# A causal convolution in 64x32 TensorE tiles, set behind the second product tile of a block

## The chip, the cores and the metric

The kernel runs on one core of one Trainium2 chip. The metric is the device time of one execution in microseconds. Three runs of the kernel before gave 463.99, 464.58 and 464.65, median 464.58. The profile is of one further execution.

The engines are named as in the profile: PE is TensorE (PEld its weight loads), DVE is VectorE, ACT is ScalarE, POOL is GpSimd, and SP issues most DMAs.

## The reference, cut to what matters

```python
# x: (8, 4160, 192)   weight: (8 heads, 7 taps)   group = 192 / 8 = 24
w = softmax(weight, axis=-1)
x_pad = concatenate([zeros((B, 6, D)), x], axis=1)
out[b, s, h, g] = sum_k w[h, k] * x_pad[b, s + k, h, g]        # a causal convolution of 7 taps
y = out.reshape(33280, 192)
h = maximum(maximum(y @ w1, y @ w2), y @ w3)                   # each w: (192, 768)
return h @ w_out                                               # w_out: (768, 192)
```

## The kernel before, in words

**Blocks.** The 33280 tokens are dealt into 65 blocks of 512. A block goes through a convolution that gives y, a first stage that gives h, and a second stage that gives the output. All matmuls are in fp16 with fp32 sums.

**First stage (`l1`, lines 499 to 504).** The maximum of three is taken as w3's product plus max(relu(first - third), second - third): `wd` holds w1 - w3 in its lower 64 rows and w2 - w3 in its upper 64. A block has six product tiles j of 128 hidden columns. For each, three matmuls of 512 columns run on the lower half of the array (rows 0 to 63, into a bank of pool `psp`, tile `lp`) and three on the upper half (rows 64 to 127, pool `psq`, tile `lq`), side by side. ScalarE takes the relu of `lp` into `r` (line 503), and VectorE takes the maximum of `r` and `lq` into `h` (line 504). Each pool has two banks.

**Second stage (`st2`, line 551).** The part of w3 that was taken out is added through `m16` = w3 @ w_out, straight from y. In each half 30 matmuls of 192 columns sum into banks of pool `psw` (four banks, tile `po`); at two places of a block ScalarE copies the lower half's sums (line 560) and VectorE adds the upper half's (line 561). The second stage of block t - 1 is dealt between the product tiles of block t, five matmuls of each half after every one, always lower, upper, lower, upper.

**Convolution.** It is made in three ways. Blocks 0 to 3 use dense matmuls (`conv_dense`, line 415, 112x32 tiles) at the start. Twelve blocks (`qpos`: 11, 16, ... 61 and 64) are made on GpSimd: cast, transposed by DMA, and summed tap by tap (`tap_q`, lines 229 to 240). All others use TensorE with a band matrix of the taps (`conv`, line 397): block 4 alone, the rest in pairs. A load (`load_x`, line 144) brings eight pieces of 70 rows (64 tokens and 6 ahead of them), GpSimd casts them (`cast_x`, line 176), and sixteen matmuls of 70 rows, 64 output tokens and 192 columns (8 heads by two column halves) write four banks, taken from `psw`, `psp`, `psw` and `psq`. Two evacuations on ScalarE and two on VectorE (line 443) copy them into `ys`. A DMA transpose for each block (`turn`, line 454) makes y with channels on partitions, and two DMAs a block (`double`, line 462) copy it to the other half of the partitions, since both halves of the array need it.

**Order.** The schedule is written by hand. In the loop over t, SP gets the load of block t + 6, the doubling of block t + 2, and later the turn of block t + 3 and the store of block t - 2. The pair (u, u + 1) is convolved in block u - 3, after that block's first product tile, behind one second-stage matmul of the lower half that is moved ahead. GpSimd gets the cast of block t + 5 and that block's share of the taps.

Of the kernel before, what the change touches and what calls it, by code (L numbers as in the profile page):

```python
# [14 lines left out]
P = 128  # L15
# [12 lines left out]
def kernel(  # L28
# [42 lines left out]
    qpos = [q for q in range(11, NB - 3, EVERY)] + [NB - 1]  # L71
# [23 lines left out]
    NR = NBLK // HALF  # L95

    def rows_of(t):
        rows = [(b, S + o) for (b, S, N, off) in blocks[t] for o in range(0, N, HALF)]
        assert len(rows) == NR
        return rows  # L100
# [4 lines left out]
    xfp = ctx.enter_context(tc.tile_pool(name="xfp", bufs=6))  # L105
# [5 lines left out]
    ydp = ctx.enter_context(tc.tile_pool(name="ydp", bufs=6))  # L111
# [9 lines left out]
    xin = {}  # L121

    def load_x(t, eng=nc.sync):
        if not 0 <= t < NB or t in qset:
            return
        pool, tag = (xfp, "xf") if t > 1 else ((xap, "xa"), (xbp, "xb"))[t]
        xf = pool.tile([P, NR, D], FP32, tag=tag, name=f"xf_{t}")
        if t < NDENSE:
            todo = [(0, c[3], c[1] * SEQ + c[2]) for c in chunks_of[t]]
        else:  # L130
            todo = [(PAD, HALF, b * SEQ) if s == 0 else (0, HALF + PAD, b * SEQ + s - PAD)
                    for b, s in rows_of(t)]
        parts = []
        i, n = 0, len(todo)
        row = [c[2] for c in todo]
        while i < n:
            k = i
            while k + 1 < n and todo[k + 1][:2] == todo[i][:2] and row[k + 1] - row[k] == row[i + 1] - row[i]:
                k += 1
            step = row[i + 1] - row[i] if k > i else 0  # L140
            p0, rlen = todo[i][:2]
            src = bass.AP(tensor=x.tensor, offset=row[i] * D,
                          ap=[[D, rlen], [step * D, k - i + 1], [1, D]])
            eng.dma_start(out=xf[p0:p0 + rlen, i:k + 1, :], in_=src)
            if parts and parts[-1][0] == rlen:
                parts[-1] = (rlen, parts[-1][1], k + 1)
            else:
                parts.append((rlen, i, k + 1))
            i = k + 1
        xin[t] = [xf, todo[0][0], parts]  # L150
# [14 lines left out]
    def cast_x(t):  # L165
# [4 lines left out]
        if u == 0:  # L170
            x16s[t0] = x16p.tile([P, NHEAD, 2, nu, NR // 2, GRP], FP16, tag="x16", name=f"x16_{t0}")
        if p0:
            nc.gpsimd.memset(xf[0:p0, 0, :], 0.0)
        K = HALF + PAD
        for c in range(2):
            nc.gpsimd.tensor_copy(out=x16s[t0][0:K, :, c, u, :, :].rearrange("p h r c -> p r h c"),  # L176
                                  in_=xf[0:K, c:NR:2, :].rearrange("p r (h c) -> p r h c", c=GRP))


# [41 lines left out]
    def tap_q(q, k):  # L221
# [17 lines left out]
        yd = dense[q] = ydp.tile([P, 2, NCH // 2, P], FP16, tag="yd", name=f"yd_{q}")  # L239
# [41 lines left out]
    for t in range(2, 7):  # L281
        load_x(t)

# [3 lines left out]
    nc.gpsimd.tensor_copy(out=ident16[:], in_=ident[:])  # L287
    idle = const.tile([P, NBLK], FP16)
# [25 lines left out]
    for v in range(2):  # L314
        nc.gpsimd.memset(xz[1][v][:], 0.0)
    wcol16 = const.tile([P, 3, KW], FP16)
# [70 lines left out]
    def conv(t, pools):  # L387
# [4 lines left out]
        per = NHEAD // n  # L392
        w = nu * (NR // 2) * GRP
        G = [pool.tile([P, per, w], FP32, tag=tag, name=f"G{i}_{t}") for i, (pool, tag) in enumerate(pools)]
        for h in range(NHEAD):
            for c in range(2):
                nc.tensor.matmul(  # L397
                    G[h // per][HALF * c:HALF * (c + 1), h % per, :],
                    lhsT=band[0:HALF + PAD, h, PAD:HALF + PAD],
                    rhs=x16s[t0][0:HALF + PAD, h, c, :, :, :].rearrange("p u r c -> p (u r c)"),  # L400
                    start=True, stop=True, tile_position=(0, HALF * c))
        slots[t0] = ysp.tile([P, nu, NR // 2, D], FP16, tag="ys", name=f"ys_{t}")
# [35 lines left out]
    def evac(t, i, copy=nc.scalar.copy):  # L438
# [3 lines left out]
        per = NHEAD // len(G)  # L442
        copy(out=slots[t][:, :, :, GRP * per * i:GRP * per * (i + 1)].rearrange(  # L443
# [3 lines left out]
    def turn(t):  # L447


        if t >= NB or t in qset:  # L450
            return
        t0, u, nu = place(t)
        yd = dense[t] = ydp.tile([P, 2, NCH // 2, P], FP16, tag="yd", name=f"yd_{t}")
        nc.sync.dma_start_transpose(out=yd[:, 0, :, :],
                                    in_=slots[t0][:, u, :, :].rearrange("p r d -> p (r d)"))

    def double(t):

        if NDENSE <= t < NB:
            yd = dense[t]  # L460
            for i in range(2):
                nc.sync.dma_start(out=yd[HALF * i:HALF * (i + 1), 1, :, :],
                                  in_=yd[HALF * (1 - i):HALF * (2 - i), 0, :, :])

    def spot(t, i, c, r):
# [3 lines left out]
        else:  # L469
            own, k = (NC * r + c) % 2, (NC * r + c) // 2  # L470
        return k + (0 if own == i else NCH // 2)

    def y_all(t, i, c):
        row = slice(HALF * i, HALF * (i + 1))
        if t < NDENSE:
            return dense[t][row, c, :]
        a = dense[t][row, 0, 0, :]
# [5 lines left out]
    def y_tok(t, i, c, s):  # L483
        row = slice(HALF * i, HALF * (i + 1))
        if t < NDENSE:
            return dense[t][row, c, P * s:P * (s + 1)]
        k = spot(t, i, c, s)
        return dense[t][row, k // 6, k % 6, :]

    def l1(t, j, pools=((psp, "p"), (psq, "q"))):  # L490


        N = blkN[t]
        ps = [pool.tile([P, NBLK], FP32, tag=tag, name=f"l{tag}{i}_{t}_{j}")
              for i, (pool, tag) in enumerate(pools)]
        for c in range(NC):
            for i in range(2):
                row = slice(HALF * i, HALF * (i + 1))
                nc.tensor.matmul(ps[i][:, 0:N], lhsT=wd[row, c, P * j:P * (j + 1)],  # L499
                                 rhs=y_all(t, i, c),  # L500
                                 start=(c == 0), stop=(c == NC - 1))
        r = rp.tile([P, NBLK], FP16, tag="r", name=f"r_{t}_{j}")
        nc.scalar.activation(out=r[:, 0:N], in_=ps[0][:, 0:N], func=AF.Relu)  # L503
        nc.vector.tensor_max(out=hs[t][:, j, 0:N], in0=r[:, 0:N], in1=ps[1][:, 0:N])  # L504

    ahead = set()

    def st2(t, u, NU, first_half_only=False):
# [5 lines left out]
        hT = hs[t]  # L514
        if t not in halves:
            todo = [[], []]
            for s in range(4):
                for i in range(2):
                    row = slice(HALF * i, HALF * (i + 1))
                    mm = [(y_tok(t, i, i, s), m16[row, 0, :])]  # L520
                    if s % 2 == i:
                        mm.append((y_tok(t, i, 2, s), m16[row, 1, :]))
                    hh = [(hT[row, j, P * s:P * (s + 1)], wo[row, j, :]) for j in range(NJ)]
                    mm = hh + mm if t == 0 else mm + hh
                    todo[i] += [(s, n == 0, n == len(mm) - 1, m) for n, m in enumerate(mm)]
# [6 lines left out]
            halves[t] = (todo, {})  # L532
        todo, ps = halves[t]
        n = len(todo[0])
        es = range(n * u // NU, n * (u + 1) // NU)
        for e in es[:1] if first_half_only else es:
            for i in range(2):
                if first_half_only:
                    if i:
                        break  # L540
                    ahead.add((t, e))
                elif i == 0 and (t, e) in ahead:
                    continue
                s, first, last, (a, b) = todo[i][e]
                b0 = s if t == NB - 1 else s - s % 2
                if (b0, i) not in ps:
                    pool, tag = (psw, "w")
                    if t == NB - 1 and s in (1, 2):
                        pool, tag = (psp, "p") if i == 0 else (psq, "q")
                    ps[b0, i] = pool.tile([P, 2, D], FP32, tag=tag, name=f"po{i}_{t}_{s}")  # L550
                nc.tensor.matmul(ps[b0, i][:, s % 2, :], lhsT=a, rhs=b, start=first, stop=last)  # L551
            ends = {todo[i][e][0] for i in range(2) if todo[i][e][2]}
            for s in sorted(ends):
                done[t, s] = done.get((t, s), 0) + sum(todo[i][e][0] == s and todo[i][e][2] for i in range(2))
                if done[t, s] < 2 or (s % 2 == 0 and t < NB - 1):
                    continue
                s0 = s if t == NB - 1 else s - 1
                ss = slice(s0 % 2, s % 2 + 1)
                a = tp.tile([P, 2, D], FP32, tag="a", name=f"a_{t}_{s}")
                nc.scalar.copy(out=a[:, ss, :], in_=ps[s0, 0][:, ss, :])  # L560
                nc.vector.tensor_add(out=outs[t][:, s0:s + 1, :], in0=a[:, ss, :],  # L561
                                     in1=ps[s0, 1][:, ss, :])
                if t == NB - 1 and s == 1:
                    store(t, 0, 2, (nc.sync,))
                elif t == NB - 1 and s == 3:
                    store(t, 2, 3, (nc.scalar,))
                    store(t, 3, 4, (nc.sync,))
# [17 lines left out]
    def begin(t):  # L585
        hs[t] = hp.tile([P, NJ, NBLK], FP16, tag="h", name=f"h_{t}")
# [168 lines left out]
```

## Time and profile before

| | |
|---|---|
| profiled execution | 464.5 us, its span 462.7 us |
| median of three runs | 464.58 us |
| granted TensorE clock | 1.00 |
| a second-stage matmul (line 551), 64x192 | 3120 and 780 of them, 243 ns as recorded |
| a first-stage matmul (line 499), 64x512 | 2316 in `lp` and `lq`, 376 ns as recorded |
| relu (line 503), maximum (line 504) | 597 ns, 686 ns |
| evacuation of the convolution (line 443) | 484 ns on ScalarE, 550 ns on VectorE, 49 each |
| GpSimd: one tap's product (229), sum (237), a cast (176) | 478 ns, 1809 ns, 822 ns |

[...] matmuls that follow each other overlap in the record: how close they start tells their cost, not how long each is. The two halves of the array are independent rows of the same timeline. The share of idle time of an engine says little unless TensorE waits for it.

### The profile page before, as it was taken

Reading aid. Unit: us, or ns where it says so; the run is one execution under the profiler, and the core shown is the slowest. Engines: PE = TensorE matmul, PEld = TensorE weight load, DVE = VectorE, ACT = ScalarE, POOL = GpSimd, SP = SyncE. Lnnn points to the kernel's source line nnn. Section 1 sums busy time; section 2 is a strip of 40 time slices with the busy share of each in tenths; the row PEclk is TensorE's granted clock in tenths of the full one; section 3 lists DMA queues with packets and bytes.
Section 4 is the critical chain, followed back from the end, with each engine's and each line's share of the span. In section 5 each row is a group of like instructions: output and inputs, shape, how many; then the busy total and the mean of one; then the engine's idle time right before and its main releaser. Section 6 shows DMA issues by size and latency. Waiting matters only on the chain.

```text
span 462.7 us, 17259 instructions
## 1 busy us (share of the span) xinstructions
PE 454.4 (98%) x6969; PEld 367.9 (80%) x6969; DVE 354.1 (77%) x595; ACT 314.3 (68%) x597; POOL 352.6 (76%) x501
## 2 busy tenths in 40 slices
PE   8999999999999999999999999999999999999997
PEld 4576788977877887888888888888888888888886
DVE  6777777777778787777878777777777777777775
ACT  5766566667676666767667676676767676676664
POOL 5753289999988978978967978978957969979500
PEclk9999999999999999999999999999999999999999
DMA  8959999999869878787789697698598797884423
GB/s 190 222 127 198 177 209 179 192 209 224 192 130 231 170 155 211 175 181 183 166 175 198 157 211 165 157 213 198 132 210 179 164 224 176 144 191 92 100 70 103
DMA packets 137527, 80.77 MB, mean 175 GB/s; under 512 B 58294, under 2 KB 137368, under 8 KB 137448
## 3 DMA queue, kind: packets, MB, share of 16 engines
q1 hardware_dynamic: 137176, 79.18, 79.1%
q8 instruction: 54, 0.88, 0.9%
q0 software_dynamic: 112, 0.39, 0.3%
q14 instruction: 25, 0.20, 0.2%
q10 hardware_dynamic: 160, 0.10, 0.1%
HBM read 29.85 MB, written 25.56 MB: 120 GB/s over the span
## 4 chain that ended last, share of the span: by engine, by line
PE 89%; POOL 5%; DMA 4%; issue 1%; DVE 0%; ACT 0%; POOLq 0%; DVEq 0%; SPq 0%
PE lq L499 35%; PE po L551 33%; PE lp L499 14%; PE G L397 4%; POOL tap L237 2%; POOL tap L229 2%; DMA yd<-ys 1%; PE idle L294 1%; DMA xt<-xq 1%; DMA yd<-yd 1%; PE D L415 1%; POOL x L176 1%; DMA xt<-xt 1%; PE lw L499 0%; PE band_cols L335 0%
## 5 line engine op out<-in xcount | busy, mean ns | idle before, releaser
L504 DVE TENSOR_TENSOR h<-r,lq 128x512 f16<-128x512 f16 x386 | 264.7, 686 | 99.5 <-ACT r L503 99.4
L503 ACT ACTIVATE r<-lp 128x512 f16<-128x512 f32 x386 | 230.5, 597 | 134.7 <-PE lp L499 123.8
L499 PE MATMUL lp<-yd,wd 64*128 64x512 f16 x1158 | 312.3, 376 | 2.2 <-DMA yd<-yd 1.6
L499 PE MATMUL lq<-yd,wd 64*128 64x512 f16 x1158 | 312.3, 376 | 0.3 <-DVE yd L431 0.3
L551 PE MATMUL po<-wo,h 64*128 64x192 f16 x3120 | 263.8, 243 | 0.7 <-issue 0.7
L551 PEld LDWEIGHTS <-h 64*128 64x128 f16 x3120 | 209.2, 94 | 22.2 <-issue 0.9
L499 PEld LDWEIGHTS <-wd 64*128 64x128 f16 x2340 | 160.9, 94 | 39.4 <-DMA yd<-yd 2.1
L176 POOL CAST x<-xf 70x768 f16<-70x768 f32 x98 | 77.8, 822 | 60.6 <-DMA xf<-in_x_dram 54.0
L229 POOL TENSOR_SCALAR tap<-xt,wcol 128x256 f32<-128x256 f16 x252 | 116.1, 478 | 3.9 <-DMA xt<-xt 3.3
L237 POOL TENSOR_TENSOR tap<-tap,tap 128x768 f32<-128x768 f32 x60 | 108.6, 1809 | 5.0
L551 PE MATMUL po<-m,yd 64*128 64x192 f16 x780 | 109.4, 243 | 0.0
L561 DVE TENSOR_TENSOR o<-a,po 128x384 f32<-128x384 f32 (+1 forms) x132 | 71.4, 541 | 1.2 <-ACT a L560 1.2
L551 PEld LDWEIGHTS <-yd 64*128 64x128 f16 x780 | 61.9, 94 | 11.8
L560 ACT COPY a<-po 128x384 f32<-128x384 f32 (+1 forms) x132 | 62.3, 473 | 3.0 <-PE po L551 3.0
L443 DVE CAST ys<-G 128x384 f16<-128x384 f32 x49 | 24.9, 550 | 0.6 <-PE G L397 0.6
L397 PEld LDWEIGHTS <-band 70*64 70x64 f16 x400 | 15.8, 109 | 9.9 <-PE lp L499 9.0
L240 POOL TENSOR_TENSOR yd<-tap,tap 128x768 f16<-128x768 f32 x12 | 21.8, 1814 | 1.0
L397 PE MATMUL G<-x,band 70*64 70x192 f16 (+1 forms) x400 | 21.2, 248 | 0.7 <-POOL x L176 0.5
L443 ACT CAST ys<-G 128x384 f16<-128x384 f32 x49 | 21.0, 484 | 0.8 <-PE G L397 0.8
L198 POOL CAST xq<-xl 128x384 f16<-128x384 f32 x24 | 11.4, 505 | 0.0
L256 POOL CAST xz<-xf 112x80 f16<-112x80 f32 (+2 forms) x18 | 5.2, 330 | 4.5 <-DMA xf<-in_x_dram 4.5
L294 PE MATMUL idle<-idle 128*128 128x512 f16 x15 | 6.4, 573 | 1.2 <-DVE idle L289 1.2
(52 smaller groups left out, 68.6 us busy)
## 6 DMA issues: line engine op xcount, KB each, us to landing
out_dram<-o SPq DMA_DIRECT2D x61, 384.0 KB
xf<-in_x_dram SPq DMA_DIRECT2D x47, 420.0 KB
yd<-yd SPq DMA_DIRECT2D x122, 96.0 KB
xl<-in_x_dram SPq DMA_DIRECT2D x12, 384.0 KB
xf<-in_x_dram SPq DMA_DIRECT2D x5, 367.5 KB
ws<-in_moe_w_dram SPq DMA_DIRECT2D x6, 192.0 KB
out_dram<-o SPq DMA_DIRECT2D x5, 192.0 KB
yd<-ys SPq DMA_TRANSPOSE x49
```

The lines of the kernel that those rows point to most:

```text
L176: nc.gpsimd.tensor_copy(out=x16s[t0][0:K, :, c, u, :, :].rearrange("p h r c -> p r h c"), in_=xf[0:K, c:NR:2, :].rearrange("p r (h c) -> p ...
L229: nc.gpsimd.tensor_scalar(out=part[:, 2 * c:2 * c + 2, :], in0=xt[:, 2 * c:2 * c + 2, LEAD - PAD + k:LEAD - PAD + k + P], scalar1=wcol[:, ...
L237: nc.gpsimd.tensor_add(out=accs[q][:], in0=accs[q][:], in1=part[:])
L240: nc.gpsimd.tensor_add(out=yd[:, 0, :, :], in0=accs.pop(q)[:], in1=part[:])
L397: nc.tensor.matmul(G[h // per][HALF * c:HALF * (c + 1), h % per, :], lhsT=band[0:HALF + PAD, h, PAD:HALF + PAD], rhs=x16s[t0][0:HALF + PAD ...
L443: copy(out=slots[t][:, :, :, GRP * per * i:GRP * per * (i + 1)].rearrange("p u r (h c) -> p h (u r) c", c=GRP), in_=G[i][:].rearrange("p h ...
L499: nc.tensor.matmul(ps[i][:, 0:N], lhsT=wd[row, c, P * j:P * (j + 1)], rhs=y_all(t, i, c), start=(c == 0), stop=(c == NC - 1))
L503: nc.scalar.activation(out=r[:, 0:N], in_=ps[0][:, 0:N], func=AF.Relu)
L504: nc.vector.tensor_max(out=hs[t][:, j, 0:N], in0=r[:, 0:N], in1=ps[1][:, 0:N])
L551: nc.tensor.matmul(ps[b0, i][:, s % 2, :], lhsT=a, rhs=b, start=first, stop=last)
L560: nc.scalar.copy(out=a[:, ss, :], in_=ps[s0, 0][:, ss, :])
L561: nc.vector.tensor_add(out=outs[t][:, s0:s + 1, :], in0=a[:, ss, :], in1=ps[s0, 1][:, ss, :])
```

## The change

- `conv`: the sixteen matmuls become 64. The array is used as 64x32 tiles: two row halves and four column quarters. A matmul now has 38 rows (32 tokens and 6 ahead of them), 32 output tokens and 96 columns for a pair of blocks. A block is loaded as sixteen pieces of 38 rows, eight on partitions 0 to 37 and eight on 64 to 101, so a load is two DMAs. The cast covers 102 partitions; the rows between are set to zero once, in six buffers that are now fixed ones.
- `turn`: two transposes for a pair, both issued behind the pair's evacuation; `double`: two DMAs for a pair instead of four. In SP's order the doubling now comes before the load.
- The convolution of a pair stands behind the second product tile. In such a block the second stage is dealt 5, 8, 4, 4, 5, 4 (`ROOM`) instead of five each: three (`OWN`) of the eight stand before the convolution in the upper half, and four more (`AHEAD`) in the lower half.
- TensorE's instructions go through two queues in the program, one for each half (`mm`, `emit`), and are written in the order in which each half becomes free, counted in columns; `meet` writes out all that is left.
- Ten GpSimd blocks (15, 20, ... 60) instead of twelve, so there are 25 pairs instead of 24.
- At the start, load 6 and the zeroing move, and `make_wd(2, 4)` comes before `l1(0, 1)`.

```diff
-    qpos = [q for q in range(11, NB - 3, EVERY)] + [NB - 1]
+    qpos = [q for q in range(15, NB - 4, EVERY)]
...
+    TOK = 32
+    NR = NBLK // TOK // 2
+    KR = TOK + PAD
...
+            if NDENSE <= t < NDENSE + XBUF:
+                nc.gpsimd.memset(xf[TOK:HALF, :, :], 0.0)
...
-            todo = [(PAD, HALF, b * SEQ) if s == 0 else (0, HALF + PAD, b * SEQ + s - PAD)
-                    for b, s in rows_of(t)]
+            todo = [(HALF * (i // NR) + (0 if s else PAD), KR if s else TOK,
+                     b * SEQ + s - (PAD if s else 0), i % NR) for i, (b, s) in enumerate(rows_of(t))]
...
-        K = HALF + PAD
-        for c in range(2):
-            nc.gpsimd.tensor_copy(out=x16s[t0][0:K, :, c, u, :, :].rearrange("p h r c -> p r h c"),
-                                  in_=xf[0:K, c:NR:2, :].rearrange("p r (h c) -> p r h c", c=GRP))
+        K = HALF + KR
+        for r in range(2):
+            nc.gpsimd.tensor_copy(out=x16s[t0][0:K, :, :, u, r, :].rearrange("p h j c -> p j h c"),
+                                  in_=xf[0:K, 4 * r:4 * r + 4, :].rearrange("p j (h c) -> p j h c", c=GRP))
...
         for h in range(NHEAD):
-            for c in range(2):
-                nc.tensor.matmul(
-                    G[h // per][HALF * c:HALF * (c + 1), h % per, :],
-                    lhsT=band[0:HALF + PAD, h, PAD:HALF + PAD],
-                    rhs=x16s[t0][0:HALF + PAD, h, c, :, :, :].rearrange("p u r c -> p (u r c)"),
-                    start=True, stop=True, tile_position=(0, HALF * c))
+            for j in range(4):
+                for i in range(2):
+                    row = slice(HALF * i, HALF * i + KR)
+                    nc.tensor.matmul(
+                        G[2 * (h // per) + i][TOK * j:TOK * (j + 1), h % per, :],
+                        lhsT=band[row, h, HALF * i + PAD:HALF * i + KR],
+                        rhs=x16s[t0][row, h, j, :, :, :].rearrange("p u r c -> p (u r c)"),
+                        start=True, stop=True, tile_position=(HALF * i, TOK * j))
...
+        for i in range(2):
+            nc.sync.dma_start_transpose(out=yp[:, 0, i, :, :, :].rearrange("p u k n -> p (u k) n"),
+                                        in_=slots[t][:, i, :, :, :].rearrange("p u r d -> p (u r d)"))
...
+    def emit(rest=False):
+        run_ops()
+        while lanes[0] or lanes[1]:
+            i = 0 if clock[0] <= clock[1] else 1
+            if not lanes[i]:
+                if not rest:
+                    return
+                i = 1 - i
+            cols, fn = lanes[i].popleft()
+            fn()
+            clock[i] += cols
+            gone[i] += 1
+            run_ops()
...
-        if t > 2 and u < NB:
-            st2(t - 1, 0, NJ, True)
-        conv(u, PQ if t == 2 else WPWQ)
...
+        cuts = ROOM if late else EVEN
+        st2(t - 1, (cuts[0], cuts[0]))
         for j in range(1, NJ):
             l1(t, j)
-            st2(t - 1, j, NJ)
+            if late and j == 1:
+                st2(t - 1, (cuts[0] + OWN + AHEAD, cuts[0] + OWN))
+                meet()
+                conv(u, WPWQ)
+                for i in (0, 2):
+                    evac(u, i)
+                for i in (1, 3):
+                    evac(u, i, nc.vector.tensor_copy)
+                turn(u)
+            st2(t - 1, (cuts[j], cuts[j]))
```

## The prediction

> **What bounds the kernel now.** I read the busy shares first, then the chain of work that ended last, then the timeline around one convolution, then the waits.
>
> ```profile
> PE 454.4 (98%) x6969; PEld 367.9 (80%) x6969; DVE 354.1 (77%) x595; ACT 314.3 (68%) x597; POOL 352.6 (76%) x501
> PE 89%; POOL 5%; DMA 4%; issue 1%; DVE 0%; ACT 0%; POOLq 0%; DVEq 0%; SPq 0%
> ```
>
> TensorE is 89% of the chain, so only a change in TensorE's own time, or a new wait in it, moves the end. The chain in order of time gives the period:
>
> ```profile
> 195.76 0.85 PE G L397 x16
> ...
> 215.84 0.85 PE G L397 x16
> ...
> 229.52 0.85 PE G L397 x16
> ...
> 251.62 0.41 PE po L551 x8
> 252.68 0.40 PE po L551 x8
> ```
>
> The second-stage groups come every 1.06 us, six to a block: 6.36 us a block. From 195.76 to 229.52 are five blocks and two convolutions: 33.76 - 5 x 6.36 = 1.96, so a convolution of a pair of blocks costs 0.98 us. Around one of them, in TensorE's timeline:
>
> ```profile
> 229.28 0.24 PE L551 MATMUL po<-m,yd 64*128 64x192 f16 x1
> 229.52 0.64 PEld L397 LDWEIGHTS <-band 70*64 70x64 f16 x16 [0.36 <-PE lp L499]
> 229.52 0.85 PE L397 MATMUL G<-x,band 70*64 70x192 f16 x16
> ...
> 230.31 0.26 PE L551 MATMUL po<-m,yd 64*128 64x192 f16 x2
> ...
> 230.40 0.49 PE L551 MATMUL po<-wo,h 64*128 64x192 f16 x7
> ```
>
> The columns are start, duration, engine, line, what is written and read, count. Two second-stage matmuls of one half start 0.08 apart (the last seven: four in one half within 0.49, less the 0.24 of the last, are three steps). Here 0.24 pass before the convolution starts, so entering it costs 0.16. Sixteen matmuls in two column halves are eight steps of 0.08 = 0.64; from 229.52 to 230.31 are 0.79, so filling and leaving cost 0.15. With 0.03 of slip between the halves that is the 0.98. Smaller shapes, and the memory side:
>
> ```profile
> 29.36 0.53 PE L397 MATMUL G<-x,band 70*64 70x96 f16 x16
> 23.01 1.10 PE L415 MATMUL D<-band,xz 112*32 112x103 f16 x60
> PE lp L499 <- DMA yd<-yd: 1.6, 2, 0.9
> PE G L397 <- POOL x L176: 0.5, 1, 0.5
> 100.00:400.00 300.00, 300.00 (x4553) 245.49 (x4550) 233.27 (x392) 207.95 (x392) 252.36 (x350) 1.00 0.83 184
> ```
>
> The lone block's convolution has 96 columns: first to last start is 0.53 - 0.21 = 0.32 for seven steps, with a slower first one, so some 0.043 a step: time goes with columns down to 96. In the dense convolution (line 415) ten groups of four column tiles and ten of two start within 1.10 - 0.21 = 0.89, or 0.046 a group of 103 columns: four tiles side by side cost hardly more than two. The waits say that TensorE waits for nothing from 100 to 400 us, and that DMA is 83% busy there.
>
> [...] Here each convolution still leaves four 128x384 tiles to be copied.
>
> **The change part by part.**
>
> *Convolution.* A pair took 16 matmuls of 192 columns, two at a time. It will take 64 of 96 columns (8 heads x 4 column tiles x 2 row halves), eight at a time: eight steps of 0.043 = 0.34 in place of 0.64. Entry and exit I keep at 0.16 + 0.15[...]. So 0.65. The step is bounded below by 0.043 (the columns) and above by 0.086 (if the eight tiles go as two fours); I take 0.043.
>
> *Its place.* It moves behind the second product tile, and eight second-stage steps instead of five stand on its two sides. Let E be the end of TensorE's stream before it. The lower half is four matmuls (0.32) ahead, so its product tile ends at E - 0.58, its result lands 0.16 later, ScalarE's relu (0.60) runs from E - 0.37 to E + 0.23, and VectorE's maximum starts at E + 0.28. VectorE's timeline of before shows what follows a maximum:
>
> ```profile
> 230.11 0.68 DVE L504 TENSOR_TENSOR h<-r,lq 128x512 f16<-128x512 f16 x1
> 230.71 1.01 DVE L443 CAST ys<-G 128x384 f16<-128x384 f32 x2
> ```
>
> The next starts 0.60 after it, and two evacuations of 0.55 take 1.01, so they follow each other by 0.46. So the evacuations start at E + 0.88 and E + 1.34, and the second ends at E + 1.89. Its bank is next wanted by the upper half's fourth product tile: convolution 0.16 + 0.34 + 0.10, five second-stage matmuls 0.42, a product tile 0.65, four more 0.33, so E + 2.0. It holds, with 0.1 to spare. ScalarE's evacuations (from E + 0.5 and E + 0.9) free the second stage's next banks at about E + 1.0 and E + 1.4, wanted at E + 1.5 by the lower half and at E + 1.8 by the upper. I allow 0.05 a convolution for a margin this thin (0 to 0.3).
>
> *Number of convolutions.* Blocks on GpSimd go from twelve to ten, so 25 pairs instead of 24. Before: 24 x 0.98 = 23.5. After: 25 x 0.70 = 17.5. Gain 6.0.
>
> *GpSimd.* One of its blocks costs (116.1 + 108.6 + 21.8 + 11.4 + 2.3) / 12 = 21.7 us; two fewer, against four more casts of 0.82 and six memsets (1.4 each, estimated from the 892 ns of a 960-element one). It stays hidden. One piece shows: block 9, counted from its first matmul of line 499, took 8.27 us where a block with a convolution takes 7.36, and the chain goes through the taps of the first GpSimd block (59.14 to 80.84) into that convolution's wait for the cast. The first such block is now 15, not 11: gain 0.9.
>
> *Halves apart.* Running the lower half ahead costs the upper one 0.32 of idleness once, at the first such convolution; after that both do equal work between two convolutions. Loss 0.3.
>
> *Loads, turns, doublings.* A load moves 16 x 38 rows of 768 bytes instead of 8 x 70: 608 packets for 560. With two blocks more, about 2,500 packets of some 47 ns over 16 engines, or 7 us of DMA time against 285: the 0.83 becomes about 0.88. Both turns of a pair are now issued together behind the evacuation, at E + 1.9 or block start + 4.0, take 1.24 each to issue on SP, and land some 2 us later (in before a doubling waiting for its turn starts 2.9 after that turn's issue began, 198.03 to 200.93); the doubling, first in SP's next block, is waiting behind them and lands by about the start of the block after, a whole block (6 us) before it is needed. SP holds back the next load behind it; GpSimd's cast waits for that load, and its taps behind the cast. GpSimd has 28.3 us of work in 33, and a finished block is due two blocks later, so I cost this at nothing; without cover it would be up to 2 us a pair. At the start it isn't free: block 5 waited in before for its doubling (0.7 of the 1.6 above). The new order puts a load and a store ahead of that turn, and takes two GpSimd loads away. I let block 5 start when it did, which gives back the gain of the two convolutions before it: loss 0.6.
>
> Sum: -6.0 - 0.9 + 0.3 + 0.6 = -6.0. The profiled execution took 464.5 (span 462.7, 1.8 around it), within 0.1 of the median of 464.58. So 458.5.
>
> **The rivals.**
>
> *Instructions are not fed fast enough (the slower side).* A convolution becomes 64 weight loads and 64 matmuls in 0.34 us, 2.7 ns each. The densest stretch in the trace, the first 40 pairs of the dense convolution, ran at 0.46 / 80 = 5.8 ns each, and there the columns were the limit, so it proves no limit. [...] The changed convolutions together equal the old 23.5 at 0.94 each, or 0.58 in the array: 4.5 ns an instruction. Beyond that the change loses. At 5.8 it is 0.74 + 0.31 + 0.05 = 1.10, 25 x 1.10 = 27.5, so +4.0 - 0.9 + 0.3 + 0.6: 468.5. For it: nothing here has shown such a rate. Against: no gap shows that feeding ever limited.
>
> *The evacuation chain is late.* If the 0.1 margin is a lack of 0.2, each convolution costs 0.25 more: 458.5 + 25 x 0.2 = 463.5. For it: VectorE is busy from E + 0.28 to about E + 3.9 without a gap. Against: VectorE is idle 0.37 before each maximum in before.
>
> *y comes late.* A doubling that misses its block by 0.4 in each pair gives 458.5 + 10 = 468.5. For it: DMA at 0.95 from 60 to 100 us. Against: 6 us of slack.
>
> *The tiles don't run eight abreast.* Two fours: 0.69 + 0.31 + 0.05 = 1.05 each, 26.3 in all, +2.8 net of the rest: 467.3. It counts with the first rival.
>
> **How the numbers follow.** Forecast 0.62 (455 to 462); feeding or two fours 0.18; evacuation 0.11; y late 0.09. Low end: no allowance, entry and exit 0.1 cheaper, start gain kept: 25 x 0.55 = 13.8, so -9.7 - 0.9 + 0.3 = 454.2. High end: 467.5 takes in the evacuation case, two fours and the milder part of feeding. About 0.2% (0.9 us) can be told from no change: faster 0.67 (the forecast and part of the evacuation case), same 0.08, slower 0.25.
>
> **What would show it.** In the new profile: G's matmuls as 64 of 96 columns within about 0.55 us, second-stage groups still 1.06 apart, 0.65 to 0.7 for a block with a convolution over 6.36, no wait of TensorE on VectorE or ScalarE after it, block 9 without its 0.9. Wrong if the G groups spread over 0.7 us or more, or if waits for yp or for the evacuation stand before product tiles.

## The result: 816.41 us, and the profile after

The changed kernel took 816.41 us (median of four runs, 815.3 to 817.25), the kernel before 464.28 beside it: a ratio of 1.758, with a 95% interval of 1.755 to 1.761. The forecast was 458.5. The profiled execution took 816.4, its span 814.6.

From the page of the changed kernel: busy shares (busy us, share of the span, instructions), the DMA row over 40 slices, in tenths, and the chain that ended last, by engine and by line:

```profile
PE 535.4 (66%) x8233; PEld 469.5 (58%) x8233; DVE 364.9 (45%) x597; ACT 315.1 (39%) x599; POOL 321.0 (39%) x450
...
DMA  8133735554554564564564555555555365354462
...
DMA 47%; PE 28%; SPq 18%; POOL 3%; issue 2%; DVE 1%; ACT 0%; POOLq 0%; DVEq 0%
DMA xf<-in_x_dram 37%; PE po L626 10%; PE lq L569 9%; DMA yp<-ys 8%; PE lp L569 7%; SPq L222 7%; SPq L165 6%; POOL x L197 3%; PE G L418 2%; SPq L492 2%; SPq L665 1%; DMA yd<-yd 1%; DMA yp<-yp 1%; SPq L347 1%; SPq L236 1%
```

TensorE was 89% of this chain and is now 28%; its granted clock is 0.80, before 1.00. The loads of x alone (`xf<-in_x_dram`) are 37% of it, 300 us. Yet the DMA engines are only about half busy. So something in the loads is slow that isn't the amount of data. The waits of the changed kernel (total us, times, longest):

```profile
POOL x L197 <- DMA xf<-in_x_dram: 368.6, 41, 16.8
...
PE G L418 <- POOL x L197: 172.4, 23, 9.2
```

and the first of these in the kernel before:

```profile
POOL x L176 <- DMA xf<-in_x_dram: 54.0, 26, 4.3
```

The row to read first is the one where TensorE waits: its convolution waits for GpSimd's cast, 172.4 us in 23 places, where it was 0.5 in one. The cast in turn waits for its load. What a load looks like while it runs is seen in the DMA view cut to 305 to 331 us, forty slices of 0.65 us each, busy tenths of 16 engines and GB/s:

```profile
DMA  0699111111111179111399112111111112357999
GB/s 0 132 184 304 36 43 44 39 46 47 46 46 47 46 165 113 46 47 47 71 341 325 46 46 72 46 47 46 47 46 45 46 46 47 74 121 180 327 345 370
```

The long stretches at 46 GB/s and one tenth busy are the loads. 46.5 GB/s are 60.5 packets of 768 bytes in a microsecond. The records of the packets give the busy share from 311.0 to 313.9 us as 0.14, which is 2.2 engines' worth out of 16: two packets are in flight at once for 81% of that time and three for the rest. Between these stretches stand bursts of over 300 GB/s at seven to nine tenths. One load DMA has 8 x 38 = 304 packets: 5.0 us at that rate, and a load has two: 10 us. Spread over 16 engines, 608 packets of 47.7 ns (their mean in the kernel before) would be 1.8, an estimate from these figures.

The timelines of GpSimd and of SyncE's queue in the same place (start, duration, engine, line, what, count, and in brackets the idle time before it and its releaser):

```profile
304.16 1.80 POOL L256 TENSOR_TENSOR tap<-tap,tap 128x768 f32<-128x768 f32 x1
305.90 0.25 POOL L194 MEMSET xf<- 6x192 f32 x1
318.17 1.59 POOL L197 CAST x<-xf 102x768 f16<-102x768 f32 x2 [12.02 <-DMA xf<-in_x_dram]
```

```profile
304.82 1.11 SPq L492 DMA_DIRECT2D yp<-yp  x2
305.97 2.72 SPq L165 DMA_DIRECT2D xf<-in_x_dram  x3
308.79 6.46 SPq L222 DMA_TRANSPOSE xt<-xq  x1
315.30 0.59 SPq L665 DMA_DIRECT2D out_dram<-o  x1
315.94 4.68 SPq L165 DMA_DIRECT2D xf<-in_x_dram  x2
```

The load issued from 305.97 is cast at 318.17; GpSimd stands idle for 12.02 us. The next is issued at 315.94, behind a transpose that holds the queue for 6.46 us, and a store. Load, cast, convolution, evacuation, turn, doubling and the next load thus form a ring through one queue, in which they stand behind each other as the timeline shows, and five blocks take 61 us (blocks 15 and 20 start at 212.74 and 274.10) instead of 33.8.

### The profile page after: what moved, and what is told of

Read it like the earlier page. It is cut to its first block, busy times and chain, and to the rows that moved or that the text cites. A ratio compares the mean times of both kernels' runs of the same rounds, so it can differ in the third digit from the quotient of the medians.

```text
span 814.6 us, 19750 instructions
## 1 busy us (share of the span) xinstructions
PE 535.4 (66%) x8233; PEld 469.5 (58%) x8233; DVE 364.9 (45%) x597; ACT 315.1 (39%) x599; POOL 321.0 (39%) x450
## 3 DMA queue, kind: packets, MB, share of 16 engines
q8 instruction: 64, 1.05, 0.5%
## 4 chain that ended last, share of the span: by engine, by line
DMA 47%; PE 28%; SPq 18%; POOL 3%; issue 2%; DVE 1%; ACT 0%; POOLq 0%; DVEq 0%
DMA xf<-in_x_dram 37%; PE po L626 10%; PE lq L569 9%; DMA yp<-ys 8%; PE lp L569 7%; SPq L222 7%; SPq L165 6%; POOL x L197 3%; PE G L418 2%; SPq L492 2%; SPq L665 1%; DMA yd<-yd 1%; DMA yp<-yp 1%; SPq L347 1%; SPq L236 1%
## 5 line engine op out<-in xcount | busy, mean ns | idle before, releaser
L626 PE MATMUL po<-wo,h 64*128 64x192 f16 x3120 | 386.1, 264 | 0.0
L569 PE MATMUL lp<-yp,wd 64*128 64x512 f16 x918 | 282.6, 416 | 51.5 <-DMA yp<-yp 49.4
L569 PE MATMUL lq<-yp,wd 64*128 64x512 f16 x918 | 277.0, 413 | 35.0 <-DVE h L577 34.5
L626 PEld LDWEIGHTS <-h 64*128 64x128 f16 x3120 | 275.0, 103 | 15.2 <-issue 0.2
L197 POOL CAST x<-xf 102x768 f16<-102x768 f32 x102 | 81.3, 825 | 446.2 <-DMA xf<-in_x_dram 368.6
L418 PE MATMUL G<-x,band 38*32 38x96 f16 (+1 forms) x1664 | 22.0, 261 | 172.4 <-POOL x L197 172.4
L626 PE MATMUL po<-m,yp 64*128 64x192 f16 x612 | 135.1, 271 | 0.0
L569 PE MATMUL lp<-yq,wd 64*128 64x512 f16 x180 | 66.4, 488 | 0.0
L626 PEld LDWEIGHTS <-yp 64*128 64x128 f16 x612 | 63.3, 105 | 1.7
L569 PE MATMUL lq<-yq,wd 64*128 64x512 f16 x180 | 63.9, 473 | 0.0
L569 PE MATMUL lq<-yd,wd 64*128 64x512 f16 x60 | 18.2, 410 | 13.1 <-DMA yd<-yd 12.9
```

The source lines that it names most:

```text
L197: nc.gpsimd.tensor_copy(out=x16s[t0][0:K, :, :, u, r, :].rearrange("p h j c -> p j h c"), in_=xf[0:K, 4 * r:4 * r + 4, :].rearrange("p j ( ...
L418: nc.tensor.matmul(G[2 * (h // per) + i][TOK * j:TOK * (j + 1), h % per, :], lhsT=band[row, h, HALF * i + PAD:HALF * i + KR], rhs=x16s[t0] ...
L569: nc.tensor.matmul(ps[i][:], lhsT=wd[HALF * i:HALF * (i + 1), c, P * j:P * (j + 1)], rhs=y_all(t, i, c), start=(c == 0), stop=(c == NC - 1))
```

## The experiments

Ratios are against the kernel before, run beside each experiment. Where a kernel has one run only, that is said.

**What is varied.** The trace shows that a load of 38 rows has 2.2 packets in flight on average, not why. That few DMA engines carry such a load (theory A below) is the author's reading of this figure; no view names the engine of a packet. So the number of rows was varied.

**1. The same rows, in pieces of 32 and 6.**

```diff
-            eng.dma_start(out=xf[p0:p0 + rlen, q0:q1, :], in_=src)
+            for lo, hi in ([(0, 32), (32, KR)] if rlen == KR else [(0, rlen)]):
...
+                eng.dma_start(out=xf[p0 + lo:p0 + hi, q0:q1, :], in_=src)
```

> The changed kernel with each load of 38 rows issued as two DMAs, of 32 and of 6 rows. Theory A (few DMA engines): in the changed kernel's trace a load in flight moves about 60 packets of 768 bytes per us[...]. Then the loads take some 2 us each again, TensorE is at full clock, and the time is that of the prediction without this fault, 455 to 466 us. Theory B (more packets, 608 for 560, and the pair's doubling ahead of the load in SP's queue): packets and order stay, so the time stays above 750 us. Theory C (TensorE's clock, 0.80 in the changed kernel, is what makes it slow): no reason for the clock to change, above 750 us.

Measured 476.23 (470.45 to 477.63), ratio 1.022 (1.013 to 1.030). The same bytes in twice as many DMAs take 340 us off. Its wait and its window (stretch, length, busy us of PE, PEld, DVE, ACT and POOL, granted clock, DMA share, GB/s):

```profile
POOL x L198 <- DMA xf<-in_x_dram: 96.0, 27, 11.4
...
PE G L419 <- POOL x L198: 3.1, 3, 1.6
```

```profile
125.00:400.00 275.00, 275.00 (x5043) 263.03 (x5040) 216.55 (x363) 192.12 (x363) 230.93 (x319) 1.00 0.88 186
```

The granted clock of its profiled run is 0.999 with no edit that bears on it, so the 0.80 came with the waits and did not make them. The DMA share of 0.88 is what the prediction expected, but that agreement says little: experiment 4, with the same loads, has 0.84 in the same window, and the page counts 137357 packets in all, where the kernel before has 137527.

**2. One row more: 39 rows in one DMA.** The source row behind the last is read too and not used.

```diff
+            read = KR + 1 if rlen == KR and len(blocks[t]) == 1 else rlen
...
-                          ap=[[D, rlen], [step * D, q1 - q0], [1, D]])
+                          ap=[[D, read], [step * D, q1 - q0], [1, D]])
```

> The changed kernel with 39 rows read where 38 are needed (the last is not used), still one DMA for each half. Theory A: [...] the time is within 2 us of the run with 32 and 6 rows. Theory D (a DMA to a narrow set of partitions is slow, whatever its number of rows): 39 rows are as slow as 38, above 750 us. Theory B: 624 packets instead of 608, slightly slower than 816 us.

Measured 483.21 (479.48 to 486.77), ratio 1.037 (1.028 to 1.045). One more row, 2.6% more bytes, takes the time from 816 to 483. It was expected within 2 us of the first experiment and is 7 us slower; some later blocks still wait for loads. What makes up these 7 us was not separated.

**3. The kernel before, with 74 rows instead of 70.** Nothing else of the change is in it.

```diff
+            read = HALF + PAD + 4 if t >= NDENSE and rlen == HALF + PAD and len(blocks[t]) == 1 else rlen
```

> The kernel before, with 74 rows read where 70 are needed (4 not used), in one DMA as it was. Theory A: [...] 592 packets at some 60 per us are 9.9 us a load, more than the 6.4 us of a block, so the old kernel becomes slow too: 650 to 820 us, with GpSimd waiting for loads. Theories B, C and D: 6% more packets in a wide DMA, 464 to 470 us.

Measured 752.86 in one run. Its DMA view from 305 to 331 us:

```profile
DMA  9712111111127722699941112111111137695117
GB/s 372 239 47 71 47 46 46 47 46 46 45 69 171 151 48 48 138 289 321 373 156 46 46 47 71 47 46 46 45 45 45 45 104 169 142 193 46 45 41 183
```

The same plateau, 46 GB/s at one tenth, in a kernel with the old convolution, the old order and the old turns. With this the cause of the slowdown is shown from both sides: the number of rows alone makes it and takes it away. That 74 rows would be slow and 39 fast was expected beforehand. That it acts through the number of engines is the author's reading of the plateau; the engines themselves were not seen, and why 38 and 74 rows run so and 39 do not was not shown.

**4. Load ahead of the doublings.** Experiment 1 was still 2.2% slower than before, and not in its steady part: from the start of block 14 to the end it takes 343.3 us, the kernel before 345.8. But block 14 starts at 122.3, before at 113.6. (A part of this can be how one run differs from another: experiment 6, the same program up to block 2, starts that block at 26.69, experiment 1 at 29.48.) So the next edits are to the order at the start. The first puts back the order of before, where SP's load stands ahead of the doublings.

```diff
+        if t > 4:
+            load_x(t + 6)
         for v in doubles_at.get(t, ...):
             double(v)
-        if t > 3:
+        if t == 4:
             load_x(t + 6)
```

> The changed kernel with loads of 32 and 6 rows, and from block 5 on the load ahead of the doubling in SP's order, as in the kernel before. In the run without this, blocks 2 to 13 lose some 9 us against before, with convolutions waiting for casts and casts for loads, while the doubling on SP waits for both turns of a pair to land. Theory S (the doubling's wait on SP holds the loads back): casts wait less for loads, blocks 6, 9 and 10 lose at most 1 us each, and the time falls by 3 to 6 us. Theory T (DMA is simply full at the start, 0.95 and more): the same bytes move in the same time, so less than 1 us of difference; putting loads ahead makes the doubling later, and it could even lose.

Measured 468.91 (463.54 to 471.76, 20 runs), ratio 1.007 (1.004 to 1.009): some 7 us better by the ratios, still not faster than before. Its profiled run, one of the slower ones (470.99), doesn't show where they come from: block 14 starts at 123.80. Blocks 9 and 10 no longer stall (6.36 and 7.15 us, where experiment 1 has 8.71 and 8.95), but blocks 3 to 5 and 13 take longer. The clock has a part in the spread of the runs: the five at a mean granted clock of 1.00 have a median of 465.65, the other fifteen 469.68; of experiment 1's four the one at 1.00 took 470.45. At the same clock that is a gain of some 5 us, with a single run on one side.

**5. The heads in the order 0, 4, 1, 5, 2, 6, 3, 7,** on experiment 1, so that neighbouring heads write different banks. In experiment 1 the pace breaks at the 33rd of 64 matmuls. If the place in the row sets it (theory F), the break stays there; if the banks do (theory P), it moves.

```diff
-        for h in range(NHEAD):
+        for h in (0, 4, 1, 5, 2, 6, 3, 7):
```

> The changed kernel with loads of 32 and 6 rows, and the heads of the convolution in the order 0, 4, 1, 5, 2, 6, 3, 7, so that its first 32 matmuls write all four banks instead of the first two. In the run without this the first 32 of a convolution's 64 matmuls start in groups of eight 0.0425 us apart, the others one by one 0.0083 apart. Theory F [...]: the pace changes at the same 33rd matmul, and the 64 start within 0.55 us again. Theory P (the second pair of banks takes results more slowly): the pace changes from the second head on, or is mixed throughout.

472.82 in one run; its convolutions answer the question. In experiment 1 the first 32 matmuls of a convolution start in groups of eight, 0.0425 us apart, as predicted (0.053 the first time), and the eight within 24 ns. Then 79 ns pass, and from the 33rd on they start one by one, 8.3 ns apart. Here the break is at the same 33rd matmul, so the bank is not its cause. What differs is the end: in experiment 1 the last two starts stand 34 ns apart, here 8. The 64 start within 0.498 instead of 0.551 us, and a convolution costs 0.75 instead of 0.79.

**6. The second stage dealt evenly, nothing ahead,** on experiment 1.

```diff
-    ROOM = [5, 13, 17, 21, 26, 30]
-    OWN, AHEAD = 3, 4
+    ROOM = EVEN
+    OWN, AHEAD = 0, 0
```

> The changed kernel with loads of 32 and 6 rows, and the second stage dealt five by five around the convolution, with no half ahead. The convolution then stands directly behind the second product tile of both halves. By the prediction's working the relu of that tile then ends 0.6 later, the second evacuation on VectorE at about E + 2.4, and its bank is wanted at E + 2.1: a block with a convolution costs 1.1 to 1.2 us over 6.36 instead of 0.79, with TensorE waiting for VectorE. Rival (the dealing doesn't matter, TensorE has slack enough in its banks): 0.79 to 0.85.

471.59 in one run. The 64 matmuls still start within 0.551, but a block with a convolution takes 7.31 to 7.36 instead of 7.15: the convolution costs 0.96 or so, as in the kernel before (0.98), and not the 1.1 to 1.2 expected. Thus the uneven dealing is worth some 0.18 a convolution, and without it the new tiles gain next to nothing. The expectation had TensorE waiting for an evacuation; the trace shows another wait, in the upper half alone (VectorE, then TensorE):

```profile
149.94 0.69 DVE L578 TENSOR_TENSOR h<-r,lq 128x512 f16<-128x512 f16 x1 [0.37 <-ACT r L577]
...
150.50 0.38 PE L570 MATMUL lp<-yp,wd 64*128 64x512 f16 x1
150.68 0.37 PE L570 MATMUL lq<-yp,wd 64*128 64x512 f16 x1
```

VectorE's maximum of the second product tile ends at 150.63. The upper half's next product tile waits for it and starts at 150.68; the lower half's starts at 150.50. The halves stay some 0.17 us apart up to the next convolution, which needs both. Here, and in the kernel before, that tile starts 53 to 55 ns after the maximum's end in every convolution from 112 us on. In experiment 1, with the uneven dealing, it starts 0.26 us or more after it, so the wait is gone. The dealing without the new tiles wasn't tried.

**7. Forty-eight rows in one DMA,** on experiment 4: one issue instead of two for each half, for 26% more packets.

```diff
-            for lo, hi in ([(0, 32), (32, KR)] if rlen == KR else [(0, rlen)]):
+            elif len(blocks[t]) == 1:
+                cut = [(0, 48)]
...
+            for lo, hi in cut:
```

> As the run with the load first, but 48 rows read where 38 are needed (10 not used) in one DMA for each half[...]: 768 packets for 608, and two DMAs a load instead of four. If [...] fewer DMAs outweigh a quarter more packets: up to 4 us faster than the run with the load first. If DMA time is what counts at the start: 2 to 6 us slower.

Measured 497.63 (495.45 to 504.9), ratio 1.077 (1.067 to 1.087), outside both expectations. Its window:

```profile
125.00:400.00 275.00, 267.83 (x4761) 250.53 (x4756) 208.74 (x348) 184.75 (x348) 220.50 (x304) 0.99 1.06 193
```

The packets' recorded times add up to 1.06 of sixteen engines, where experiment 4 has 0.84 in the same window: the amount is the likely cause. So fewer issues alone weren't enough here.

**8. Loads early.** Before block 2 SP waits some 7 us (from 25.6 to 32.7 in experiment 4) for the dense convolution of block 3, and all its later loads stand behind that wait. Loads 7 to 10 are now issued ahead of that point and all later ones a block earlier, on experiment 4.

```diff
-    get_x(7)
+    load_x(7)
+    load_x(8)
...
+    load_x(9)
     cast_x(4)
+    load_x(10)
...
-        if t > 4:
-            load_x(t + 6)
+        if t > 3:
+            load_x(t + 7)
```

> The version with loads of 32 and 6 rows and the load ahead of the doublings, and now the loads of blocks 7 to 10 are issued before block 2 (SyncE stands idle there from 25.6 to 32.7 us waiting for block 3's dense convolution) and every later load one block earlier. Theory (what is still lost against the kernel before is SyncE's issuing at the start, four transfers a load, behind the turns): blocks 3 to 6 and 13 lose their stalls (together 6.7 us against the kernel before), GpSimd no longer waits for loads of blocks 7 to 9, and the time is 457 to 461, ratio 0.985 to 0.995. Rival (the start is bound by the number and shape of the transfers themselves, by the DMA engines): the stalls move but stay, 464 to 470.

Measured 462.67 (461.5 to 464.3, 14 runs), ratio 0.9988 (0.9976 to 1.0): some 4 us better than experiment 4 by the ratios, and short of the 457 to 461 expected. It is 0.8 less than before beside it, but the interval reaches 1.0, so it isn't shown to be faster. Block 14 starts at 114.99, and from block 5 on no block loses more than 0.1 us.

**9. The same early loads in the kernel before.**

```diff
+    load_x(7)
+    load_x(8)
...
+    load_x(9)
     cast_x(4)
+    load_x(10)
...
-        if t > 4:
-            load_x(t + 6)
+        if t > 3:
+            load_x(t + 7)
```

> The kernel before with the same edit to its order of loads alone. It separates what the earlier loads bring by themselves from what the change brings. If only the changed kernel is short of SyncE time at the start, it stays within 0.3% of the kernel before, or gains up to 1 us from the stall of block 9 (0.93 us). If the earlier loads are worth as much here, 458 to 461, and the gain of the changed version is not the convolution's.

Measured 467.6 (466.76 to 469.67), ratio 1.010 (1.008 to 1.013): slower, which neither reading expected. It loses 6.4 us in block 2, which takes 14.33 us instead of 7.97; blocks 3, 4 and 9 gain 1.3, 1.0 and 0.9. The cross-half copies of block 3 are issued later than before, behind eight loads, but in this trace TensorE does not wait for them. It stops inside the convolution of block 4 (TensorE's timeline, then its window):

```profile
28.90 0.45 PE L397 MATMUL G<-x,band 70*64 70x96 f16 x12
32.57 0.37 PE L397 MATMUL G<-x,band 70*64 70x96 f16 x4 [3.22 <-issue]
```

```profile
32.50:38.00 5.50, 5.43 (x48) 3.53 (x49) 1.37 (x3) 1.20 (x2) 3.64 (x6) 0.50 1.20 206
```

For 3.22 us TensorE waits for nothing that the profile shows, and then, until about 38.7, it runs at a granted clock of 0.50: matmuls of 512 columns start 0.42 us apart instead of 0.21. Together these make up nearly all of the 6.4. All six runs have a mean clock of 0.992 to 0.996. What stops TensorE wasn't tested. One lead: in the records of DMA packets, a 16 KB transfer of the instruction queue (q8) lands at 31.02, 1.6 us before the stop ends. In the traces of both kernels and all experiments together, TensorE has nine stops of over 0.6 us put down to "issue", and each ends 1.3 to 2.4 us after such a landing. That the instructions came late is the author's reading of these records, with the DMA share at 1.05 from 29 to 32.5 us; it was not shown.

So the kernel before doesn't gain from the same edit. Whether a gentler one would keep the 3.2 us of blocks 3, 4 and 9 without the stop wasn't tried, so the later ratios don't say how far the new convolution alone beats a kernel before with its best order.

**10. Early loads and alternating heads together** (5 and 8).

```diff
-        for h in range(NHEAD):
+        for h in (0, 4, 1, 5, 2, 6, 3, 7):
```

> The version with early loads, and the heads of the convolution in the order 0, 4, 1, 5, 2, 6, 3, 7. In an earlier run that order made a convolution 0.75 instead of 0.79 us; 20 or so of them lie in blocks that no other wait hides, so 0.5 to 1.0 us faster than the version with early loads alone. If the order is worth nothing, equal within 0.1%.

Measured 461.59 (459.17 to 463.89, 16 runs), ratio 0.9964 (0.9946 to 0.9981), the fastest in ratio and below 1 with its whole interval, which overlaps that of experiment 8. Its busy shares, and TensorE's timeline around one convolution:

```profile
PE 451.1 (98%) x8233; PEld 418.1 (91%) x8233; DVE 358.6 (78%) x597; ACT 314.7 (69%) x599; POOL 319.1 (69%) x450
```

```profile
89.80 0.41 PE L627 MATMUL po<-wo,h 64*128 64x192 f16 x5
89.97 0.24 PE L627 MATMUL po<-m,yp 64*128 64x192 f16 x1
90.14 0.71 PE L419 MATMUL G<-x,band 38*32 38x96 f16 x64
90.78 0.25 PE L627 MATMUL po<-wo,h 64*128 64x192 f16 x1
90.78 0.25 PE L627 MATMUL po<-m,yp 64*128 64x192 f16 x1
```

From 89.97, the last second-stage matmul, to 90.14 are 0.17: less one step of 0.08, the entry costs 0.09. From 90.14 to the second stage again are 0.64, of which the starts take 0.50. From block 14 to the end this run takes 341.6 us, before 345.8. VectorE in the same place:

```profile
90.29 0.69 DVE L578 TENSOR_TENSOR h<-r,lq 128x512 f16<-128x512 f16 x1 [0.37 <-ACT r L577]
90.90 1.02 DVE L466 CAST ys<-G 128x384 f16<-128x384 f32 x2
92.35 0.69 DVE L578 TENSOR_TENSOR h<-r,lq 128x512 f16<-128x512 f16 x1 [0.43 <-ACT r L577]
```

The two evacuations end at 91.92, and VectorE then waits 0.43 for the next relu. The upper half's fourth product tile, which takes the bank of the second, starts at 92.19. From 125 to 400 us TensorE is busy throughout in this run too, with no wait on an evacuation.

**11. A convolution cut in two,** on experiment 8: 32 matmuls, then second-stage matmuls of 192 columns, then the other 32.

```diff
         for h in range(NHEAD):
+            if h == 4:
+                between()
...
+                def between():
+                    st2(t - 1, (cuts[1], cuts[1]))
+                    meet()
```

> The version with early loads, but each convolution of a pair is cut after 32 matmuls, with second-stage matmuls of 192 columns between the halves. It is not meant to be faster (two more entries and exits). Feeding theory (TensorE has some 32 pairs of weight load and matmul ready while it is busy with wide matmuls, and is fed one pair in 8.3 ns when they are used up): both halves run at 0.0425 us per eight, each 32 start within 0.17 to 0.19 us. Rival (the later heads are slower for another reason, the bank or the place they write or their data): the second half starts at 8.3 ns each, 32 within 0.25 to 0.27 us.

473.6 in one run, where experiment 8 took 462.67; what makes up the difference wasn't separated. TensorE's timeline:

```profile
93.37 0.36 PE L422 MATMUL G<-x,band 38*32 38x96 f16 x32
93.67 0.25 PE L629 MATMUL po<-wo,h 64*128 64x192 f16 x1
93.67 0.25 PE L629 MATMUL po<-m,yp 64*128 64x192 f16 x1
93.76 0.49 PE L629 MATMUL po<-wo,h 64*128 64x192 f16 x4
94.18 0.36 PE L422 MATMUL G<-x,band 38*32 38x96 f16 x32
```

Both halves take 0.36 with the last matmul's own 0.2, so each 32 start within 0.16 us, eights 0.043 apart. The second 32 are the heads 4 to 7, the very matmuls that come at 8.3 ns each when nothing stands between. So neither their data nor their bank slows them. In experiment 10, 33 weight loads and 32 matmuls of a convolution start at the pace of 0.0425 us for eight; the next weight load comes 105 ns later, and from there a weight load and a matmul alternate, 4.2 ns an instruction. This fits the feeding theory, which is the author's: what was measured is that the first 32 pairs behind wide matmuls start at 5.3 ns a pair and later ones at 8.3; what holds or feeds them was not seen. The pause isn't explained by it. If 32 ready pairs were used at 5.3 ns each and new ones came every 8.3 all the while, they would last beyond the 64th pair (an estimate from these two paces: 32 x 8.3 / 3.0 = 89), so by this theory the new ones come late. Why, and whether another limit on 32 small matmuls in a row would look the same, stays open.

**12. Only two loads early,** blocks 9 and 10 behind the cross-half copies, on experiment 10. There TensorE had waited 1.26 us for these copies in block 3.

```diff
-    load_x(9)
     cast_x(4)
-    load_x(10)
...
+            load_x(9)
             turn(4)
+            load_x(10)
```

> As the version with early loads and alternating heads, but only blocks 7 and 8 are loaded ahead of block 3's cross-half copies on SyncE; block 9 follows these copies and block 10 the first turn. In the version with four early loads TensorE waited 1.26 us in block 3 for these copies (issued at 34.68 and 35.41 us, behind 28 load transfers), and the kernel before with four early loads was 1.0% slower. If that wait is the price of the early loads, it goes, and the time is 1 to 2 us under that version: 459 to 461, ratio 0.990 to 0.995. Rival (loads 9 and 10, now late, cost as much in blocks 4 to 6): the same 461 to 463.

Measured 462.08 (458.06 to 464.15, 22 runs), ratio 0.997 (0.9953 to 0.9988), the same as experiment 10 within the intervals. In its profiled run the wait for the copies is gone, but TensorE waits 1.2 us for a doubling. Runs of one kernel spread by 3 to 6 us here, those of the kernel before too, so single runs don't rank these versions. The clock has a part in it: the nine runs at a mean clock of 1.00 have a median of 461.46, the other thirteen 462.9. The rest wasn't found: block 0 starts at 11.33 us in experiment 10 and at 9.72 here, with the same program up to there.

## Why the prediction was wrong, step by step

- **"Loads, turns, doublings": the step that failed.** It priced the loads as "about 2,500 packets of some 47 ns over 16 engines" and said "I cost this at nothing". A load's cost was taken from its number of packets; the shape of 38 rows made it 10 us a load instead of some 2: the 304 packets of a DMA went by at 60.5 in a microsecond, with 2.2 in flight on average. (The sum has a slip as well: 7 us on 285 is 2.5%, which makes 0.83 about 0.85, not 0.88.) The page of before had the transfers of 70 rows only, so the profile couldn't show the fall; the shape was in the diff, and the step priced it as if it ran like one of 70 rows. The step did say what goes wrong when a load is late ("GpSimd's cast waits for that load"), but gave it 2 us a pair, where the wait of TensorE alone came to 172.4 us in 23 places.
- **The other half of the same step, the start.** "Loss 0.6" was 8.7 us in the profiled run of experiment 1 (block 14 at 122.3 instead of 113.6), of which up to 3 can be how one run differs from another. This includes the price of the cure, since four DMAs a load instead of two occupy SP for 1.8 us. In experiment 8 block 14 starts at 115.0: the order of SP's queue alone got most of it back. The price of the cure wasn't separated from the order.
- **"Convolution": mis-sized.** 0.65 and an allowance of 0.05 became 0.79 (0.75 with the heads alternating). Entry and exit were cheaper, 0.09 and some 0.14 against 0.16 + 0.15. The step of eight was exact for the first half, 0.0425 against 0.043. What was too low are the 64 starts, 0.55 or 0.50 instead of 0.34: a pause of 0.08 before the 33rd matmul, and 8.3 ns for each after it. This is the rival on feeding in a milder form, just under its break-even of 0.58; its case of 5.8 ns an instruction was too high. So 25 x 0.79 = 19.8 in place of 17.5: a gain of 3.8, not 6.0.
- **"Its place": held, but not by 0.1.** No TensorE wait on an evacuation stands in the steady part, and the rival of a late evacuation falls. In experiment 10 E, the end of TensorE's stream before the convolution, is 90.05 (89.97 and one step). The second evacuation ends at E + 1.87, where the working had 1.89. The bank is next used at E + 2.14 and not at 2.0, because the convolution takes longer than planned; so a margin of 0.1 was never tried. Experiment 6 adds what the prediction didn't see: the dealing is worth 0.18 a convolution, nearly all that it became cheaper by, since it takes away a wait for VectorE's maximum.
- **"y comes late": falls for the steady part.** Between 125 and 400 us TensorE waits for no doubling in experiments 1 and 10. In the changed kernel it waits 49.4 us for doublings, as a part of the ring.
- **"GpSimd": held where it can be seen.** Block 9 takes 6.36 in experiments 4 and 10, without the 0.9. In experiment 1 it was covered by the stalls of the start. Earlier loads alone remove it too (experiment 9).
- **Two fours instead of eights: refuted** by the first 32 starts.
- **The sum, without the fault of the loads.** From block 14 on both kernels have 19 convolutions: 19 x (0.98 - 0.75) = 4.4, less 0.27 for a longer last block, is 4.1; measured 345.8 - 341.6 = 4.2. Over the whole run experiment 10 gains 1.9 by the medians. Its profiled run is behind at the start: block 3 starts at 38.04, before at 35.54. The forecast of 6.0 took both the convolution and the start as too cheap.

## What to carry to other kernels

When an edit changes the row count of a DMA, measure a DMA of the new shape before you price it by its bytes: 38, 39 and 32 + 6 rows of the same data took 816, 483 and 476 us. Here a low DMA share together with long waits for DMA was the sign of it, and a flat plateau of 46 GB/s, with 2.2 engines' worth of packet time, pointed to how few packets were in flight and not to how many there were. When a convolution or any small product is cut into more and smaller matmuls, count the instructions: past the first 32 pairs here a pair of 96 columns cost 8.3 ns instead of 5.3. Breaking the run up by wide matmuls brought the pace back, but not the time: experiment 11 took 473.6 us in its one run, experiment 8 462.67. And see what the halves of the array wait for around such a run: here the dealing of the work beside it was worth more than the tiles.

## What the runs showed that was not expected

- A load DMA of 38 or 74 rows, each in pieces of 768 bytes, runs at 46 GB/s, and one added row or a cut into 32 and 6 brings the time down by 333 to 340 us.
- TensorE starts a weight load and a matmul of 96 columns in 64x32 tiles every 5.3 ns (eight in 0.0425 us) for the first 32 pairs, and, after a pause of 79 ns, every 8.3 ns for the rest.
- The order of heads changes the last two starts of a convolution by 26 ns each; its reason stays open.
- A convolution became 0.19 us cheaper with the new tiles and the uneven dealing, 0.02 with the tiles alone. The kernel before has the same wait of the upper half for VectorE's maximum.
- The same early loads made the version with loads of 32 and 6 rows 0.8% faster and the kernel before 1.0% slower: in the latter TensorE stops for 3.2 us and then runs at half its clock for some 6.8.
